# Attention units ahead of two mixture stages: other banks, bias engines and issue order in the first twenty units

## The chip, the cores and the metric

The kernel runs on one core of a Trainium2 chip. The metric is the device time of one execution in microseconds (us). The program is launched once; loads from HBM and the write of the result count.

## The reference, cut to what matters

Three layers follow each other. The change touches the first and the start of the second.

```python
# 1. attention: 4 batches, 8 heads, 576 positions, 64 wide, window 128, ALiBi bias
scores = q @ k.T / 8 + bias[h]            # bias[h] = -slope[h] * distance, masked outside the window
attn = exp(scores - max); attn /= sum(attn) + 1e-9
x = (attn @ v)                            # becomes 2304 tokens x 512
# 2. gated layer
x = (sigmoid(x @ w_gate) * (x @ w_val)) @ w_out        # 512 -> 1536 -> 512
# 3. top-1 mixture of 8 experts
out = gate_w * (relu(x @ w1[e]) @ w2[e])
```

## The kernel before, in words

The attention is cut into 36 **units**: a unit is two heads (one pair `g`) by two blocks of 128 tokens (`b`, `b+1`). The chunks of tokens are 2, 4, 4, 4 and 4 blocks (`CHUNKS`), so units 0 to 3 are chunk 0, units 4 to 11 chunk 1, units 12 to 19 chunk 2, and so on. A unit goes through these functions:

- `unit_s` (line 204): eight score products into two banks of tag `s`, then for each of four slices z VectorE adds the bias and takes the row's minimum (L225), and ScalarE takes the exponential with its sum (L228).
- `unit_n` (line 232): VectorE makes the reciprocal of the sums (L238, L239), and GpSimd scales the four slices (L108); for units 0 and 1 VectorE takes half of them (L106).
- `unit_t` (line 245): TensorE transposes the scaled slices into two banks (L255), and two copies take them to SBUF (`tt`): ScalarE the one of u = 0 (L96), VectorE the one of u = 1 (L98).
- `unit_b` (line 274): the products with v go to one bank `o` (L288); a copy (`xf`, VectorE for units below 11 and ScalarE from then on) takes the result to SBUF.
- `bias_of` (line 148) makes a head's bias tile from `relm` when it is first asked for, by a ScalarE multiplication (L154). `make_edge` (line 185) builds, for the units that hold a batch's edge, four masked copies of bias tiles on GpSimd (L100 and L201).

There are eight PSUM banks: two of tag `s`, two of `t`, three of `m` and one of `o`. In the first twenty units (`NA = 20`) transposes use `t` and the product with v uses `m`. From unit 20 on the product with v uses the single bank `o`, and `m` belongs to the gated layer.

The gated layer is computed for the pairs of chunks by seven products each (`seven`, line 392: m1 to m7 on sums and differences of blocks of x and of the weights), and for chunk 0 ("rest") by two classical products, `rg` (gate) and `rv` (value) in `rest_mm` (L451), of twelve matmuls each. Every operand is split into a high and a low part: a ScalarE copy (L96), then a VectorE subtraction (L112). Weights arrive as 64-bit words and are turned into float32 by one ScalarE and three VectorE instructions per half (L116, L122, L123, L125), then summed (L353 to L356) and split.

The order of the work: `with tc.manual_schedule(engines=...)` makes the named engines issue in source order; the engines that are not named get their order from the framework's scheduler, which sees the dependences and the source's order as a priority. Lines 491 to 514 name TensorE, VectorE, ScalarE and GpSimd. Twelve idle products (`warm`, L493) come first, then units 0 to 2, then a loop over i = 0 to 20 in which iteration i issues `unit_t(i)`, `unit_b(i-1)`, `unit_n(i+2)`, `make_edge(i+5)`, `unit_s(i+3)`, loads, and whatever the table `AT` holds for i: from i = 5 on the splits, sums and weight conversions of the gated layer. From line 540 on, for units 20 to 35, only TensorE is named; each iteration also runs some steps of the gated layer, taken from the list `todo` (line 517), each with the weight work (`after`) that follows it. SP issues the loads and has an order of its own throughout.

Of the kernel before, what the change touches and what calls it, by code (L numbers as in the profile page):

```python
# [15 lines left out]
ALU = mybir.AluOpType  # L16
# [5 lines left out]
B, H, S, D = 4, 8, 576, 64  # L22
# [5 lines left out]
P = 128  # L28
# [3 lines left out]
KF = FF // P  # L32
# [11 lines left out]
NWARM = 12  # L44
CHUNKS = [2, 4, 4, 4, 4]
PAIRS = [(2, 1), (4, 3)]
NA = 20
LEAD = 3
UB = 5
STEPS = [2, 4, 4, 5] + [5] * 12  # L50

# [2 lines left out]
def attn_ffn_moe(ctx: ExitStack, tc: tile.TileContext, qd, kd, vd, wgv, w_out, emb, tau, w1, w2, cst, ids, out):  # L54
    nc = tc.nc
# [15 lines left out]
    def pt(tag, name, bufs):  # L71
        return ps.tile([P, 512], F32, tag=tag, name=name, bufs=bufs)
# [9 lines left out]
    relm = cs[:, 0:256]  # L82
# [65 lines left out]
    def bias_of(h):  # L148
        while len(bias_t) <= h:
            z = len(bias_t)  # L150
            if z % 4 == 0:
                bias_c.append(slot([P, 4, 256], F32, f"bias{z}"))
            t = bias_c[-1][:, z % 4, :]
            nc.scalar.mul(t, relm, -8.0 * 2.0 ** (-8.0 * (z + 1) / H))  # L154
            bias_t.append(t)
        return bias_t[h]

# [5 lines left out]
    def load_qk(i):  # L163
        if i >= NU or i in qk_t:
            return
        c, b, g = units[i]
        lo = 0 if b else P
        q = ap.tile([P, 256], F32, tag="q", name=f"q{i}", bufs=UB)
        k = ap.tile([P, 384], F32, tag="k", name=f"k{i}", bufs=UB)
        nc.sync.dma_start(q, qd[:, g, b * P:b * P + 256])  # L170
        nc.sync.dma_start(k[:, lo:384], kd[:, g, (b - 1) * P + lo:(b + 2) * P])
        qk_t[i] = (q, k)
# [31 lines left out]
    def unit_s(i):  # L204
        if i >= NU or i in has_s:
            return
        has_s.add(i)
        c, b, g = units[i]
        fks = [first_key(b + j) for j in range(2)]
        halves = [slice(u * D, u * D + D) for u in range(2)]  # L210
        q, k = qk_t[i]
        ss = [pt("s", f"s{i}_{u}", 2) for u in range(2)]
        for j, f in enumerate(fks):
            for u in range(2):
                nc.tensor.matmul(ss[u][:, j * 256 + f:j * 256 + 256], q[halves[u], j * P:(j + 1) * P],  # L215
                                 k[halves[u], j * P + f:j * P + 256], start=True, stop=True)
        p = ap.tile([P, 4, 256], F32, tag="p", name=f"p{i}", bufs=4)
        mx = ap.tile([P, 4], F32, tag="mx", name=f"mx{i}", bufs=4)
        su = ap.tile([P, 4], F32, tag="su", name=f"su{i}", bufs=4)
        for u in range(2):  # L220
            for j, f in enumerate(fks):
                z = 2 * u + j
                bias = edge.pop((i, u, j), None)
                bias = bias_of(2 * g + u) if bias is None else bias
                nc.vector.tensor_tensor_reduce(  # L225
                    out=p[:, z, f:], in0=ss[u][:, j * 256 + f:j * 256 + 256], in1=bias[:, f:],
                    scale=-0.125, scalar=3.0e38, op0=ALU.add, op1=ALU.min, accum_out=mx[:, z:z + 1])
                nc.scalar.activation(out=p[:, z, f:], in_=p[:, z, f:], func=AF.Exp, scale=-1.0,  # L228
                                     bias=mx[:, z:z + 1], accum_out=su[:, z:z + 1])
        fst[i] = (p, fks, su)  # L230
# [14 lines left out]
    def unit_t(i):  # L245
        p, fks, su = fst[i]
        tts = []
        for u in range(2):
            t = pt("t", f"t{i}_{u}", 2)
            tt = ap.tile([P, 512], F32, tag="pt", name=f"tt{i}_{u}", bufs=4)  # L250
            runs = []
            for j, f in enumerate(fks):
                for o in range(f, 256, P):
                    a = j * 256 + o
                    nc.tensor.transpose(t[:, a:a + P], p[:, 2 * u + j, o:o + P], ident)  # L255
                    if runs and runs[-1][1] == a:
                        runs[-1][1] = a + P
                    else:
                        runs.append([a, a + P])
            for a, z in runs:  # L260
                hi_copy("v" if u and i < NA else "a", tt[:, a:z], t[:, a:z])
            tts.append(tt)
        fst[i] = (tts, fks)
# [10 lines left out]
    def unit_b(i):  # L274
        c, b, g = units[i]
        tts, fks = fst.pop(i)
        v = v_t.pop(i)
        o = pt("m", f"o{i}", 3) if i < NA else pt("o", f"o{i}", 1)
        mms = []
        for kb in range(-1, 2):  # L280
            q0, q1 = max(kb, 0), min(kb + 2, 2)
            if kb < 1 and fks[kb + 1]:
                q1 = min(q1, kb + 1)
            if q1 > q0:
                mms.append((kb, q0, q1, (kb + 1 + q0) * P))
        for z, (kb, q0, q1, c0) in enumerate(mms):
            for u in range(2):
                nc.tensor.matmul(o[u * D:u * D + D, q0 * P:q1 * P], v[:, kb + 1, u * D:u * D + D],  # L288
                                 tts[u][:, c0:c0 + (q1 - q0) * P], start=(z == 0), stop=(z == len(mms) - 1),
                                 skip_group_check=True)  # L290
        x = x_of(c, b, g)
        return lambda: hi_copy("v" if i < 11 else "a", x, o[:, 0:256])
# [14 lines left out]
    def builds(pair):  # L307
        one, two = PAIRS[pair]

        def src(half, k):  # L310
            return xf[PAIRS[pair][half], k]

        return {
            "S1+": lambda: sum_x((pair, "S1"), src(1, 0), src(1, 1), ALU.add),
            "S3+": lambda: sum_x((pair, "S3"), src(1, 0), src(0, 0), ALU.subtract),
            "S2+": lambda: sum_x((pair, "S2"), xf[pair, "S1"], src(0, 0), ALU.subtract),
            "S4+": lambda: sum_x((pair, "S4"), src(0, 1), xf[pair, "S2"], ALU.subtract),
            "A11": lambda: split_x((pair, "A11"), src(0, 0)),
            "A12": lambda: split_x((pair, "A12"), src(0, 1)),
            "A22": lambda: split_x((pair, "A22"), src(1, 1)),  # L320
            "S1": lambda: split_x((pair, "S1"), xf[pair, "S1"]),
            "S2": lambda: split_x((pair, "S2"), xf[pair, "S2"]),
            "S3": lambda: split_x((pair, "S3"), xf[pair, "S3"]),
            "S4": lambda: split_x((pair, "S4"), xf[pair, "S4"]),
        }
# [43 lines left out]
    def split_w(pair, f, z):  # L369
        if f < KF:  # L370
            t = (wf, tf)[z].pop(f)
            h_, l_ = (wide([P, 2 * KD, P], f"w{y}{pair}{z}_{f}", pair or f < 10) for y in "hl")
            hi_copy("a", h_, t)
            lo_sub("v", l_, t, h_)
            for q, name in enumerate((("B11", "B21", "B12", "B22"), ("T1", "T2", "T3", "T4"))[z]):
                wq[pair, f, name] = (h_[:, 2 * q:2 * q + 2], l_[:, 2 * q:2 * q + 2])
# [98 lines left out]
    wp = pt("o", "warm", 1)  # L475
# [3 lines left out]
    def latest(*engines):  # L479
        traced = nc.cur_bb.bb.instructions  # L480
        return [next(i for i in reversed(traced) if i.engine == e) for e in engines]

    bA = builds(0)
    AT = {
        5: [lambda: split_x("rest", xf.pop((0, 0)))],
        12: [bA["S1+"]], 13: [bA["A22"], lambda: load_w(0)], 14: [bA["S1"], lambda: conv_w(0, 0)],
        15: [lambda: conv_w(0, 1), lambda: load_w(1)], 16: [lambda: sum_w(0)],
        17: [bA["A11"], lambda: split_w(0, 0, 0)], 18: [bA["S3+"], lambda: split_w(0, 0, 1)],
        19: [bA["S3"], bA["S2+"]], 20: [bA["S2"]],
    }  # L490
    with tc.manual_schedule(engines={ENG.PE, ENG.DVE, ENG.Activation, ENG.Pool}):
        for _ in range(NWARM):
            nc.tensor.matmul(wp, warm[:, 0:P], warm, start=True, stop=True)  # L493
        unit_s(0)
        unit_s(1)
        load_qk(4)
        load_qk(5)
        unit_n(0)
        unit_s(2)
        load_qk(6)  # L500
        unit_n(1)
        for i in range(NA + 1):
            if i < NA:
                unit_t(i)
            if i:
                unit_b(i - 1)()
                load_v(i + 3)
            if i < NA:
                unit_n(i + 2)
                make_edge(i + 5)  # L510
                unit_s(i + LEAD)
                load_qk(i + LEAD + 4)
            for t in AT.get(i, []):
                t()
# [1 line left out]

    todo = []
    for f in range(KF):
        s = seven(0, f, "mmm", True)
        steps = [s[z] for z in "m1 m2 m5 m6 rg m7 rv m4 m3".split()]  # L520
        if f == 0:
            steps = [s[z] for z in "m1 m5 rg m6 rv m7 m2 m4 m3".split()]
        after = {0: lambda f=f: load_w(f + 2), 1: lambda f=f: conv_w(f + 1, 0), 3: lambda f=f: conv_w(f + 1, 1),
                 4: lambda f=f: sum_w(f + 1), 5: lambda f=f: split_w(0, f + 1, 0), 7: lambda f=f: split_w(0, f + 1, 1)}
        for z, t in enumerate(steps):
            todo.append((t, after.get(z)))

# [620 lines left out]
```

## Time and profile before

| what | value |
|---|---|
| median of 3 runs | 864.5 us (863.77 to 866.05) |
| profiled execution, its own time | 864.99 us |
| its span, first to last instruction | 863.1 us |
| mean granted TensorE clock | 0.981 of full speed |
| TensorE busy | 824.4 us (96%) |
| VectorE busy | 552.7 us (64%) |
| ScalarE busy | 459.7 us (53%) |
| GpSimd busy | 174.9 us (20%) |
| DMA | 140.39 MB, 163 GB/s in the mean |

The span is what the instructions cover; the time of the execution is 1.9 us more. In the trace PE is TensorE's matmuls, PEld its weight loads, DVE VectorE, ACT ScalarE, POOL GpSimd and SP the queue that issues loads. Busy time of PE is modelled, since matmuls overlap, so it is an upper bound of its work. The granted clock is given as a share of 2.4 GHz; 0.5 is the lower of its two levels, 1.2 GHz.

### The profile page before, as it was taken

How to read it: one execution, taken by the hardware profiler on the slowest of the kernel's cores; microseconds unless marked ns; L12 is line 12 of the kernel's file. 1: busy time of each engine (PE TensorE's matmuls, PEld its weight loads, DVE VectorE, ACT ScalarE, POOL GpSimd, SP SyncE). 2: the span in 40 equal slices, each digit the busy share in tenths (PEclk: the TensorE clock that was granted, in tenths of full speed). 3: DMA queues.
4: the chain of work that ended last, by engine and by line, in shares of the span. 5: the costliest groups of instructions: out<-in, count | busy, mean ns of one | idle time of the engine just before them, and what ended most of it. 6: DMA issues, size and time to landing. Idle time of an engine off the chain costs nothing. (4 is left out here: it accounts for less than half of the span.)

```text
span 863.1 us, 13488 instructions
## 1 busy us (share of the span) xinstructions
PE 824.4 (96%) x4616; PEld 663.7 (77%) x4616; DVE 552.7 (64%) x1367; ACT 459.7 (53%) x937; POOL 174.9 (20%) x275
## 2 busy tenths in 40 slices
PE   7896889999999999999999999999999999999997
PEld 4664567788788888888777777777878989878885
DVE  4887798768678778778944445564745545545553
ACT  5785776667556456566654445554344334333331
POOL 2773652323200000000000101111221221320210
PEclk7997899999999999999999999999999999999999
DMA  5557466645256356666625544414456544444520
GB/s 176 149 164 227 119 214 223 221 165 201 80 204 219 128 197 228 215 235 227 221 62 153 163 130 122 122 50 111 158 172 205 176 164 170 156 156 151 178 78 17
DMA packets 72455, 140.39 MB, mean 163 GB/s; under 512 B 8984, under 2 KB 38296, under 8 KB 72386
## 3 DMA queue, kind: packets, MB, share of 16 engines
q1 hardware_dynamic: 68482, 129.41, 46.0%
q0 software_dynamic: 3904, 10.12, 3.7%
q8 instruction: 37, 0.61, 0.3%
q14 instruction: 32, 0.26, 0.1%
HBM read 103.23 MB, written 36.93 MB: 162 GB/s over the span
## 5 line engine op out<-in xcount | busy, mean ns | idle before, releaser
L725 PE MATMUL y<-wo,gh 128*128 128x512 f32 x432 | 141.6, 402 | 0.0
L108 POOL TENSOR_SCALAR p<-p,rs 128x256 f32<-128x256 f32 (+1 forms) x140 | 81.4, 600 | 131.5 <-DVE rs L239 72.9
L905 PE MATMUL h<-xe,weh 128*128 128x256 f32 (+4 forms) x512 | 105.8, 301 | 1.5 <-DVE h L908 1.5
L921 PE MATMUL z<-weh,h 128*128 128x512 f32 (+3 forms) x320 | 103.0, 399 | 0.0
L725 PEld LDWEIGHTS y<-wo,gh 128*128 128x128 f32 x432 | 79.9, 188 | 20.3 <-issue 3.3
L228 ACT ACTIVATE p<-p,mx 128x256 f32<-128x256 f32 (+1 forms) x144 | 69.9, 486 | 39.7 <-DVE mx L225 39.5
L112 DVE TENSOR_TENSOR wel<-wer,weh 128x1024 fp32r<-128x1024 f32 x64 | 78.1, 1223 | 20.1 <-ACT weh L96 19.8
L905 PEld LDWEIGHTS h<-xe,weh 128*128 128x128 f32 x512 | 83.2, 188 | 4.2 <-DVE h L908 2.7
L725 PE MATMUL y<-wo,gl 128*128 128x512 f32 x216 | 85.8, 398 | 0.0
L907 ACT ACTIVATE h<-h 128x256 fp32r<-128x256 f32 (+4 forms) x64 | 26.6, 417 | 96.6 <-PE h L905 95.0
L905 PE MATMUL h<-xe,wel 128*128 128x256 f32 (+4 forms) x256 | 76.2, 299 | 0.3 <-DVE wel L112 0.2
L96 ACT CAST weh<-wer 128x1024 fp32r<-128x1024 f32 x64 | 66.2, 1048 | 8.3 <-DMA wer<-in_w 8.2
L921 PEld LDWEIGHTS z<-weh,h 128*128 128x128 f32 (+3 forms) x320 | 56.7, 180 | 15.0
L921 PE MATMUL z<-wel,h 128*128 128x512 f32 (+3 forms) x160 | 63.2, 395 | 0.0
L926 POOL DMA_INDIRECT out<-y,cols x19 | 25.0, 1315 | 172.0 <-DVE y L925 159.9
L255 PE MATMUL t<-cs,p 128*128 128x128 f32 x272 | 41.6, 294 | 13.6 <-ACT tt L96 6.9
L908 DVE SCALAR_TENSOR_TENSOR h<-h,h 128x256 fp32r<-128x256 f32 (+4 forms) x64 | 29.6, 464 | 38.0 <-ACT h L907 37.8
L925 DVE TENSOR_SCALAR y<-z,xg 128x512 f32<-128x512 f32 (+3 forms) x22 | 16.5, 749 | 57.4 <-PE z L921 54.2
L255 PEld LDWEIGHTS t<-cs,p 128*128 128x128 f32 x272 | 32.8, 150 | 24.8 <-issue 16.4
L819 POOL DMA_INDIRECT tab_d<-ids_sb,ai x18 | 18.3, 1017 | 163.1 <-DVE ai L816 139.6
L741 ACT ACTIVATE xr<-y 128x512 f32<-128x512 f32 x18 | 10.8, 598 | 76.0 <-PE y L725 68.7
L215 PE MATMUL s<-k,q 64*128 64x256 f32 (+1 forms) x288 | 46.1, 428 | 3.9 <-DVE mx L225 3.9
(327 smaller groups left out, 1949.4 us busy)
## 6 DMA issues: line engine op xcount, KB each, us to landing
wer<-in_w SPq DMA_DIRECT2D x64, 512.0 KB, 4.7
gl<-gT_d SPq DMA_DIRECT2D x27, 512.0 KB, 6.1
wr<-in_wgv SPq DMA_DIRECT2D x24, 512.0 KB, 5.2
gT_d<-c SPq DMA_DIRECT2D x48, 256.0 KB, 2.1
k<-in_kd SPq DMA_DIRECT2D x32, 192.0 KB, 2.8
v<-in_vd SPq DMA_DIRECT2D x32, 192.0 KB, 2.4
wf_d<-wf SPq DMA_DIRECT2D x12, 512.0 KB, 2.7
tf_d<-tf SPq DMA_DIRECT2D x12, 512.0 KB, 2.9
```

The costliest lines, as they stand in the source:

```text
L96: nc.scalar.copy(o, i)
L108: nc.gpsimd.tensor_scalar(out=t, in0=t, scalar1=r, scalar2=0.0, op0=ALU.mult, op1=ALU.add)
L112: e.tensor_tensor(out=o, in0=i, in1=h.bitcast(F32), op=ALU.subtract)
L215: nc.tensor.matmul(ss[u][:, j * 256 + f:j * 256 + 256], q[halves[u], j * P:(j + 1) * P], k[halves[u], j * P + f:j * P + 256], start=True, ...
L228: nc.scalar.activation(out=p[:, z, f:], in_=p[:, z, f:], func=AF.Exp, scale=-1.0, bias=mx[:, z:z + 1], accum_out=su[:, z:z + 1])
L255: nc.tensor.transpose(t[:, a:a + P], p[:, 2 * u + j, o:o + P], ident)
L725: nc.tensor.matmul(m, g[:, k % 4, u * P:(u + 1) * P], w[:, k % 3, :], start=(k == 0 and z == 0), stop=(k == KF - 1 and z == 2))
L905: nc.tensor.matmul(m[:, :n], w[:, fs], x[:, k, :], start=(cnt == 0), stop=(cnt == 3 * KD - 1))
L907: nc.scalar.activation(out=hh, in_=m[:, :n], func=AF.Relu)
L908: nc.vector.scalar_tensor_tensor(out=hl, in0=m[:, :n], scalar=0.0, in1=hh.bitcast(F32), op0=ALU.max, op1=ALU.subtract)
L921: nc.tensor.matmul(m[0:w, :], h, ww[:, ds], start=(cnt == 0), stop=(cnt == 3 * KE - 1))
L926: nc.gpsimd.indirect_dma_start(out=out, out_offset=IOA(ap=idx[0:w], axis=0), in_=y[0:w, :], in_offset=None, bounds_check=NT - 1, oob_is_er ...
```

## The change

Five edits are made, all in the attention units and at the start of the gated layer.

1. Transposes of the odd units below 20 take their two banks from tag `m` (three banks); even units keep `t`. The product with v takes the single bank `o` in every unit.
2. All eight bias tiles are made ahead of unit 0: head 0's on ScalarE, head 1's on VectorE, heads 2 to 7 on GpSimd.
3. Fourteen more idle products stand behind the scores of units 0, 1 and 2 (4, 4 and 6), into the bank `o` that the twelve first ones use.
4. `rg` and `rv` of the gated layer's first weight block move from the list `todo` (units 21 and 22) to iterations 19 and 20. The list has two steps fewer, and the weight work that hung on them hangs on their neighbours.
5. From iteration 10 (`SPLIT`) to 20 only TensorE and GpSimd issue in source order; VectorE and ScalarE are ordered by the scheduler there, as they were from unit 20 on.

```diff
+SPLIT = 10
...
-            nc.scalar.mul(t, relm, -8.0 * 2.0 ** (-8.0 * (z + 1) / H))
+            s = -8.0 * 2.0 ** (-8.0 * (z + 1) / H)
+            if z == 0:
+                nc.scalar.mul(t, relm, s)
+            elif z == 1:
+                nc.vector.tensor_scalar_mul(t, relm, s)
+            else:
+                nc.gpsimd.tensor_scalar(out=t, in0=relm, scalar1=s, scalar2=0.0, op0=ALU.mult, op1=ALU.add)
...
-            t = pt("t", f"t{i}_{u}", 2)
+            t = pt("m", f"t{i}_{u}", 3) if i < NA and i % 2 else pt("t", f"t{i}_{u}", 2)
...
-        o = pt("m", f"o{i}", 3) if i < NA else pt("o", f"o{i}", 1)
+        o = pt("o", f"o{i}", 1)
...
+    sA = [seven(0, f, "mmm", True) for f in range(KF)]
...
-        19: [bA["S3"], bA["S2+"]], 20: [bA["S2"]],
+        19: [bA["S3"], bA["S2+"], sA[0]["rg"]], 20: [bA["S2"], sA[0]["rv"]],
...
-        for _ in range(NWARM):
-            nc.tensor.matmul(wp, warm[:, 0:P], warm, start=True, stop=True)
+        def keep_warm(n):
+            for _ in range(n):
+                nc.tensor.matmul(wp, warm[:, 0:P], warm, start=True, stop=True)
+
+        keep_warm(NWARM)
+        bias_of(H - 1)
         unit_s(0)
+        keep_warm(4)
         unit_s(1)
+        keep_warm(4)
         load_qk(4)
         load_qk(5)
         unit_n(0)
         unit_s(2)
+        keep_warm(6)
         load_qk(6)
         unit_n(1)
-        for i in range(NA + 1):
+        for i in range(SPLIT):
...
+    with tc.manual_schedule(engines={ENG.PE, ENG.Pool}):
+        for i in range(SPLIT, NA + 1):
...
-            steps = [s[z] for z in "m1 m5 rg m6 rv m7 m2 m4 m3".split()]
+            steps = [s[z] for z in "m1 m5 m6 m7 m2 m4 m3".split()]
...
+        if f == 0:
+            after = {z: after[y] for z, y in enumerate((0, 1, 3, 4, 5, 7))}
```

The two loops hold the same calls as the one loop before.

## Rows read from the trace of the kernel before

**Rows 1.** The profile's first two parts: busy time, and the span in 40 slices.

```profile
PE 824.4 (96%) x4616; PEld 663.7 (77%) x4616; DVE 552.7 (64%) x1367; ACT 459.7 (53%) x937; POOL 174.9 (20%) x275
...
PE   7896889999999999999999999999999999999997
...
PEclk7997899999999999999999999999999999999999
```

**Rows 2.** Stretches: length, busy time and instructions of PE, PEld, DVE, ACT, POOL; clock, DMA.

```profile
0.00:20.00 20.00, 14.87 (x60) 8.31 (x62) 8.54 (x52) 11.38 (x39) 4.33 (x14) 0.79 0.63 187
20.00:50.00 30.00, 26.81 (x222) 18.66 (x218) 24.42 (x103) 22.01 (x78) 23.61 (x63) 0.97 0.49 143
50.00:97.00 47.00, 36.57 (x276) 25.31 (x274) 35.97 (x131) 32.63 (x110) 23.46 (x48) 0.82 0.60 184
97.00:115.00 18.00, 14.47 (x106) 10.90 (x105) 14.53 (x38) 13.35 (x32) 10.35 (x17) 1.00 0.43 128
115.00:180.00 65.00, 61.76 (x383) 49.24 (x383) 52.65 (x136) 44.55 (x110) 22.40 (x41) 0.97 0.67 222
180.00:863.00 683.00, 669.95 (x3579) 551.27 (x3577) 416.57 (x915) 335.75 (x571) 90.72 (x94) 1.00 0.48 157
```

**Rows 3.** The same view for two stretches at the lower clock.

```profile
12.30:22.20 9.90, 9.87 (x43) 6.51 (x43) 6.48 (x31) 6.55 (x26) 5.75 (x15) 0.53 0.39 116
69.00:79.70 10.70, 8.26 (x48) 5.55 (x45) 6.63 (x24) 7.45 (x24) 3.19 (x8) 0.52 0.71 223
```

**Rows 4.** The bias tiles: all of L154, one wait in the timeline, all such waits.

```profile
L154 ACT ACTIVATE bias<-cs x8: 398/400/416, 4.9 to 19.0; 128x256 f32<-128x256 f32 x8
...
8.31 0.29 DVE L225 CUSTOM_DVE_ANT_0 p<-s,bias 128x128 f32<-128x128 f32 x1 [1.01 <-ACT bias L154]
...
DVE p L225 <- ACT bias L154: 5.1, 5, 1.0
```

**Rows 5.** The timeline of POOL from unit 2's scaling to unit 10's, and its groups there.

```profile
17.96 1.64 POOL L108 TENSOR_SCALAR p<-p,rs 128x128 f32<-128x128 f32 x4 [0.54 <-DVE rs L239]
...
45.58 3.69 POOL L108 TENSOR_SCALAR p<-p,rs 128x256 f32<-128x256 f32 x8
...
L108 POOL TENSOR_SCALAR p<-p,rs 128x256 f32<-128x256 f32 (+1 forms) x36 | 16.2, 472 | 4.6 <-PE t L255 2.5 <-DVE rs L239 2.1
L100 POOL TENSOR_SCALAR edge<-bias 128x256 f32<-128x256 f32 x16 | 6.5, 408 | 0.7
L201 POOL MEMSET edge<- 64x192 f32 (+1 forms) x16 | 3.2, 203 | 0.9
```

**Rows 6.** Idle products at the start: weight loads, in the timeline.

```profile
4.15 0.15 PEld L493 LDWEIGHTS <-warm 128*128 128x128 bf16 x1 [0.28 <-issue]
...
4.58 0.57 PEld L493 LDWEIGHTS <-warm 128*128 128x128 bf16 x3 [0.28 <-issue]
```

**Rows 7.** Transposes of units 5, 10 and 20 in the timeline; their group, 50.3 to 97.1.

```profile
31.43 1.09 PE L255 MATMUL t<-cs,p 128*128 128x128 f32 x8 [0.16 <-ACT tt L96]
...
50.31 1.06 PE L255 MATMUL t<-cs,p 128*128 128x128 f32 x8 [0.19 <-ACT tt L96]
...
97.11 0.66 PE L255 MATMUL t<-cs,p 128*128 128x128 f32 x4
...
L255 PE MATMUL t<-cs,p 128*128 128x128 f32 x72 | 12.4, 308 | 10.4 <-ACT tt L96 4.5 <-DVE rs L238 4.0 <-issue 1.5
```

**Rows 8.** Unit 23 in the timeline: its scores, its scaling, and unit 21's product with v.

```profile
103.17 1.14 PE L215 MATMUL s<-k,q 64*128 64x256 f32 x8
...
111.80 4.11 POOL L108 TENSOR_SCALAR p<-p,rs 128x256 f32<-128x256 f32 x4 [6.87 <-DVE rs L239]
111.91 1.09 PE L288 MATMUL o<-tt,v 128*64 128x128 f32 x12 [2.31 <-ACT xf L96]
```

**Rows 9.** Two neighbouring matmuls of `rg` in the timeline.

```profile
106.72 0.28 PE L451 MATMUL r<-xl_rest,wh 128*128 128x256 f32 x1
...
106.84 0.28 PE L451 MATMUL r<-xh_rest,wl 128*128 128x256 f32 x1
```

More of the change, by code (lines that the diff above doesn't have):

```diff
@@ L499, in attn_ffn_moe @@
         unit_s(2)
+        keep_warm(6)
         load_qk(6)
         unit_n(1)
-        for i in range(NA + 1):
+        for i in range(SPLIT):
+            if i < NA:
+                unit_t(i)
+            if i:
+                unit_b(i - 1)()
+                load_v(i + 3)
+            if i < NA:
+                unit_n(i + 2)
+                make_edge(i + 5)
+                unit_s(i + LEAD)
+                load_qk(i + LEAD + 4)
+            for t in AT.get(i, []):
+                t()
+    with tc.manual_schedule(engines={ENG.PE, ENG.Pool}):
+        for i in range(SPLIT, NA + 1):
             if i < NA:
@@ L518, in attn_ffn_moe @@
     for f in range(KF):
-        s = seven(0, f, "mmm", True)
+        s = sA[f]
         steps = [s[z] for z in "m1 m2 m5 m6 rg m7 rv m4 m3".split()]
         if f == 0:
-            steps = [s[z] for z in "m1 m5 rg m6 rv m7 m2 m4 m3".split()]
+            steps = [s[z] for z in "m1 m5 m6 m7 m2 m4 m3".split()]
         after = {0: lambda f=f: load_w(f + 2), 1: lambda f=f: conv_w(f + 1, 0), 3: lambda f=f: conv_w(f + 1, 1),
                  4: lambda f=f: sum_w(f + 1), 5: lambda f=f: split_w(0, f + 1, 0), 7: lambda f=f: split_w(0, f + 1, 1)}
+        if f == 0:
+            after = {z: after[y] for z, y in enumerate((0, 1, 3, 4, 5, 7))}
         for z, t in enumerate(steps):
```

## The prediction, made before the changed kernel was run

> **What bounds the kernel now.** I read the page's slices first, then the time by stage, then the timeline of the weak stages. TensorE is busy 824.4 of 863.1 us, and the slices show that the missing part lies at the front, where the granted clock dips too [rows 1]. By stage: before 115 us PE is busy 92.7 of 115 us and idle 22.3; in the 65 us behind it idles 3.2, and from 180 us on 13 in 683 [rows 2]. So behind 115 us the kernel is bound by TensorE and what remains is a fixed amount of work: a microsecond by which that stage begins earlier is a microsecond off the end, unless DVE, busy 52.7 of 65 us there, can't keep up. All five edits lie ahead of that point. Two stretches at the lower clock add to the loss: around 17 us PE is busy 9.87 of 9.9 us at a clock of 0.53, around 74 us 8.26 of 10.7 at 0.52 [rows 3]; behind gaps in PE's work, both.
>
> Durations are those of the profiled execution, 864.99 us; the median is 0.5 less. I sum against 865.0 and take 0.5 off. A measurement of this kernel tells 0.3%, 2.6 us, from no change.
>
> **The start: biases, idle products and banks, up to unit 10.** ScalarE makes eight biases of 0.40 us, one at a time between its exponentials, and VectorE's first score of a head waits 1.01 us for one, 5.1 us in five waits [rows 4]. Made ahead, six of them cost POOL 0.41 each by its like instruction of the same shape, 2.5 us [rows 5], in a stretch where it is busy 4.3 of 20 us [rows 2]; the one on VectorE I bound by nothing and by ScalarE's 0.40, beside its wait for the first scores, and take nothing. The first of the five waits ends at 8.31, the last stands near 19; four lie ahead of unit 2's scaling at 17.96. They are 4 x 1.01 = 4.0 us of a chain in which scores, exponentials and the next unit's scores follow each other, so that scaling should start near 14.0.
>
> From there to unit 10's scaling POOL is the chain: it ends at 45.58 + 3.69 = 49.27, 31.3 us for 16.2 + 6.5 + 3.2 = 25.9 us of work, idle 5.4 [rows 5]. A part of it is what the new banks go at: transposes held by the last unit's ScalarE copy (PE's matmul 0.16 to 0.19 us in units 5 and 10 [rows 7]), since with two banks the next unit can't begin before both copies, and the scores and products queued behind them on PE. Four banks in turn take that wait away; the single `o` is late next, but below unit 10 its copy stands on VectorE ahead of the next scores, and one unit's transposes lie between. I let half of the idle time go, 2.5 us, so the start is worth 6.5 us. Upper bound: 4.0 with all of POOL's idle time but 1.6, 7.8. Lower bound: the fourteen idle products. The weight loads of the first ones stand 0.43 us apart, the last three lie within 0.57 us together, 0.19 each [rows 6]. At 0.19 they are 2.7 us, in the 5.1 us that PE is idle in the first 20 [rows 2]; at 0.43 they are 6.0, stand ahead of units 1's and 2's scores and of unit 0's transposes, and the 3.4 us more come off the 4.0. With no gain in POOL's idle time either, 0.6 is left. I take the quick price, since the twelve first ones end on it.
>
> **Free order, iterations 10 to 20.** Units 10 to 20 take 97.1 - 50.3 = 46.8 us [rows 7], 4.68 a unit where units 5 to 10 took (50.3 - 31.4) / 5 = 3.8. VectorE is busy 36.0 us of it and ScalarE 32.6 [rows 2]: in source order the splits and conversions stand as blocks between units, each engine waits for the other's half, and PE's transposes wait 10.4 us in sum [rows 7]. Freed, the blocks fill holes. What it can give at most is VectorE's idle time, 47.0 - 36.0 = 11 us. What it costs shows in unit 23, in the stage where both engines are free already: from its scores at 103.17 to the end of its scaling at 111.80 + 4.11 = 115.9 it takes 12.7 us [rows 8], because splits go between its four slices. Scores run three units ahead, so such a unit allows a period of 12.7 / 3 = 4.24 us: 42.4 in place of 46.8, a gain of 4.4. I take 4.5, the end nearer to a row of the very mechanism; the range keeps 0 and 11. The SP loads of q, k and v are tied to PE's order and not moved.
>
> In that unit POOL's four scalings take 4.11 us where the mean of four is 4 x 0.47 = 1.9 [rows 5, 8]. Without the stretch the unit's chain would be 10.5 us and the period 3.5: a gain of 11.7, VectorE's whole bound.
>
> By the Trainium skill, page "SBUF — State Buffer", section "Who interferes with whom", a VectorE instruction with two SBUF inputs and a GpSimd one that reads SBUF exclude each other for a whole instruction. By that the stretch stays wherever splits are put beside scalings, and the sum goes by 4.5 and not by 11; the stretched row agrees, and it speaks against this edit.
>
> **rg and rv.** Their 24 matmuls stand 0.12 us apart [rows 9], 2.9 us of PE's work, moved from between products of unit 21 and 22 into iterations 19 and 20. PE is idle 3.5 us from 97 to 115 [rows 2]. Where they go they fill gaps; where they were they covered the wait for the splits of S2 and S3, which m6 and m7 now meet at once. So between 0 and 2.9; I take 1. The weight work moves with the steps and changes no engine's total.
>
> **Sum.** 6.5 + 4.5 + 1 = 12 us: 865.0 - 12 - 0.5 = **852.5 us**. By the lower ends (0.6, 0, 0) 864, by the upper ones (7.8, 11, 2.9) 843.
>
> **Rivals.**
>
> *POOL holds the free units.* If each scaling is stretched to 4.11 us and the edges of units 21, 23, 25 and 27 come beside them, built in iterations 16, 18, 20 and 22, POOL has 2 x 4.11 + 2.8 = 11 us for two units, 5.5 a unit. (Four edges are 4 x (0.41 + 0.20) = 2.4 by the groups, 2.8 with gaps [rows 5].) Units 16 to 19 then lose 4 x (5.5 - 4.24) = 5 us, and the free part gives nothing: 865 - 6.5 - 1 - 0.5 = 857; with the start at its lower bound 863. For it: one row of 4.11. Against it: POOL is busy only 23.5 of 47 us there [rows 2].
>
> *The one bank o makes it slower.* From unit 11 on the copy that frees `o` is ScalarE's; freed, it may stand behind exponentials and splits. In the stage where that is so already, PE waits 2.31 us for it with unit 21's product [rows 8]. PE issues in source order, so the next scores and transposes queue behind the waiting product. Ten units of that are 23.1 us; the 10.4 us that PE idles now [rows 7] absorb a part, 12.7 remain. With the start's 6.5 kept and no other gain: 865 + 12.7 - 6.5 - 0.5 = 871. It turns slower than before once the waits exceed the present idle time by 9 us (6.5 + 2.6), 0.9 a unit. Against it: with little to fill in, the copy is short and old in the source's order, and only some waits behind 97 us are of that size.
>
> *The order doesn't change.* The scheduler, following source priority, may give nearly the old order between 50 and 97 us: the free part is then nothing, 857.
>
> *VectorE fills wholly.* Its bound of 11 us is nearly reached: 843 to 846.
>
> **Chances and range.** The forecast, 846 to 857: 0.55. POOL, 857 to 863: 0.25, of which 0.05 lies within 0.3%. Order unchanged, 857: 0.05. VectorE filled: 0.03. One bank: 0.12, of which 0.02 within 0.3%. So faster by over 0.3%: 0.55 + 0.20 + 0.05 + 0.03 = 0.83; within: 0.07; slower: 0.10. The range reaches over the forecast and POOL's case, a little above its upper end and the sum's lower bounds: 844 to 864. Left out are the bank's case and part of VectorE's.
>
> **What would show it.** In the changed profile the waits of VectorE for a bias should be gone, unit 2's scaling should start near 14 us and unit 10's end near 42.8; the granted clock should stay at its upper level between 10 and 22 us. Unit 20's transposes should start near 97.1 - 11 = 86 us, and the work behind 115 us should be the same, begun some 12 us earlier. Wrong would be: a clock of 0.5 in the start with the idle products 0.43 apart; scalings of 4 us throughout iterations 10 to 20; waits of PE's product with v on the copy of `o`, ten times over; or an early start that the stage behind 115 us loses again in waits of PE on VectorE.

## The result and the profile after

The changed kernel takes 853.32 us in the median of four runs (852.27 to 854.88), the kernel before beside it 864.83 (863.77 to 866.05): a ratio of 0.9866 with a 95% interval of 0.9847 to 0.9884, 11.5 us less. 852.5 was forecast, in a range of 844 to 864. The sum came out; several of its terms did not, and the experiments below take them apart. The profiled execution after is the slowest of the four, 854.88 us with a span of 852.9.

The page of the changed kernel, the parts that answer to [rows 1]:

```profile
PE 827.9 (97%) x4630; PEld 663.3 (78%) x4630; DVE 550.7 (65%) x1368; ACT 456.4 (54%) x930; POOL 184.3 (22%) x281
...
PE   9998898999999999999999999999999999999997
...
PEclk9999899999999999999999999999999999999999
```

The hole at the front is smaller, and of the clock's dips one still shows in the slices. The time by stage of the changed kernel, with the columns of [rows 2]:

```profile
0.00:20.00 20.00, 18.78 (x107) 10.19 (x108) 11.92 (x66) 11.59 (x43) 9.11 (x29) 1.00 0.73 214
20.00:50.00 30.00, 28.23 (x215) 18.98 (x213) 23.30 (x98) 21.17 (x73) 22.95 (x59) 0.94 0.48 143
50.00:97.00 47.00, 43.36 (x314) 30.30 (x314) 38.28 (x138) 37.38 (x120) 32.21 (x54) 0.89 0.58 187
97.00:115.00 18.00, 15.66 (x88) 11.27 (x86) 15.76 (x39) 13.23 (x32) 7.80 (x15) 1.00 0.56 179
```

Before 115 us PE is busy 106.0 in place of 92.7 us, and the clock of the first 20 us is 1.00 in place of 0.79. The whole of the first 180 us in one row each, for the kernel before, the changed kernel and e5, the changed kernel without two of its edits (below):

```profile
0.00:180.00 180.00, 154.47 (x1039) 112.43 (x1040) 136.11 (x452) 123.93 (x367) 84.16 (x181) 0.91 0.59 186
...
0.00:180.00 180.00, 168.42 (x1114) 120.38 (x1115) 140.53 (x467) 127.00 (x368) 97.40 (x191) 0.96 0.60 193
...
0.00:180.00 180.00, 164.43 (x1141) 119.73 (x1142) 145.19 (x479) 131.52 (x382) 98.22 (x199) 0.99 0.63 199
```

Milestones of the changed kernel from its timeline, beside [rows 5, 7]: unit 2's scaling, unit 10's scaling, then the first transposes of units 10 and 20 and the second half of unit 20's:

```profile
15.22 1.63 POOL L109 TENSOR_SCALAR p<-p,rs 128x128 f32<-128x128 f32 x4 [0.54 <-DVE rs L246]
...
43.55 1.84 POOL L109 TENSOR_SCALAR p<-p,rs 128x256 f32<-128x256 f32 x4 [0.57 <-DVE rs L246]
...
46.26 0.33 PE L262 MATMUL t<-cs,p 128*128 128x128 f32 x1
...
83.55 0.48 PE L262 MATMUL t<-cs,p 128*128 128x128 f32 x1
...
92.28 0.71 PE L262 MATMUL t<-cs,p 128*128 128x128 f32 x4
```

In the kernel before, unit 19's first transposes and the second half of unit 20's:

```profile
90.45 0.87 PE L255 MATMUL t<-cs,p 128*128 128x128 f32 x3 [2.40 <-ACT tt L96]
...
98.59 0.63 PE L255 MATMUL t<-cs,p 128*128 128x128 f32 x4
```

Unit 2's scaling comes 2.7 us earlier, unit 10's ends 49.27 - 45.39 = 3.9 earlier, its transposes start 4.0 earlier. Unit 20's first transposes start 13.6 earlier, but that is not the same point of the work: where the order is free, half of them are issued ahead of and among unit 22's scores, and the kernel before issues them behind. Their second half starts 98.59 - 92.28 = 6.3 earlier, with `rg` now ahead of it as a product that before stood later. Three places in this trace lose again. In the first, between 34 and 40 us, unit 7's transposes run at once, and PE then has nothing until the product with v of unit 6 can go. From the timeline:

```profile
33.25 1.29 PE L262 MATMUL t<-cs,p 128*128 128x128 f32 x8
36.16 1.09 PE L295 MATMUL o<-tt,v 128*64 128x128 f32 x12 [1.61 <-issue]
37.18 2.70 PE L222 MATMUL s<-k,q 64*128 64x256 f32 x8
39.81 1.77 PE L262 MATMUL t<-cs,p 128*128 128x128 f32 x8
...
35.65 0.41 DVE L99 COPY xf<-o 128x256 f32<-128x256 f32 x1
```

Two stretches of 2 us around it, with the columns of [rows 2]:

```profile
34.00:36.00 2.00, 0.55 (x4) 0.20 (x2) 2.00 (x4) 0.27 (x1) 0.05 (x1) 1.00 0.62 191
...
38.00:40.00 2.00, 2.00 (x7) 1.17 (x8) 1.79 (x9) 1.58 (x6) 1.79 (x6) 0.50 0.33 98
```

The product starts 0.10 us after the copy `xf` that frees the one bank `o` (35.65 + 0.41 = 36.06). PE is busy 0.55 of the 2 us ahead, and from 38 to 40 us the granted clock is 0.50: the scores behind take 2.70 us and the next transposes 1.77, where 1.14 and 1.09 are their times elsewhere at the upper level [rows 7, 8]. In the second place POOL is late, and `rg` runs behind it at the lower clock. The timeline, and then the stretch around it:

```profile
78.14 6.29 POOL L109 TENSOR_SCALAR p<-p,rs 128x256 f32<-128x256 f32 x8
...
81.64 0.33 PE L262 MATMUL t<-cs,p 128*128 128x128 f32 x1 [0.87 <-POOL p L109]
...
88.32 0.41 PE L458 MATMUL r<-xl_rest,wh 128*128 128x256 f32 x1
...
88.54 0.42 PE L458 MATMUL r<-xh_rest,wl 128*128 128x256 f32 x1
```

```profile
83.00:93.00 10.00, 10.00 (x48) 7.09 (x45) 6.33 (x16) 5.68 (x15) 6.65 (x11) 0.53 0.18 54
```

Eight scalings take 6.29 us, 3.1 for four where [rows 5] have 1.9; `rg`'s matmuls stand 0.21 us apart where [rows 9] have 0.12, in a stretch with a clock of 0.53. The third place is m7's first matmul, which waits for ScalarE's copy of the bank that m6 filled, a wait that the same matmul does not have in the trace of before (115.5 us), where `rv` stands between them:

```profile
103.97 0.50 PE L392 MATMUL a<-xh_(0, 'S3')_1349,wh 128*128 128x512 f32 x1 [2.22 <-ACT r L432]
```

### The profile page after: what moved, and what is told of

It is laid out like the page before. It is cut to its first block, busy times and chain, and to the rows that moved or that the text cites. A ratio compares the mean times of both kernels' runs of the same rounds, so it can differ in the third digit from the quotient of the medians.

```text
span 852.9 us, 13498 instructions
## 1 busy us (share of the span) xinstructions
PE 827.9 (97%) x4630; PEld 663.3 (78%) x4630; DVE 550.7 (65%) x1368; ACT 456.4 (54%) x930; POOL 184.3 (22%) x281
## 5 line engine op out<-in xcount | busy, mean ns | idle before, releaser
L109 POOL TENSOR_SCALAR p<-p,rs 128x256 f32<-128x256 f32 (+1 forms) x140 | 88.4, 649 | 111.0 <-DVE rs L246 35.9
L952 PEld LDWEIGHTS z<-weh,h 128*128 128x128 f32 (+3 forms) x320 | 56.7, 180 | 14.9
L936 PEld LDWEIGHTS h<-xe,wel 128*128 128x128 f32 x256 | 48.1, 188 | 0.7 <-DVE wel L113 0.7
L232 DVE CUSTOM_DVE_ANT_0 p<-s,bias 128x256 f32<-128x256 f32 (+1 forms) x112 | 40.0, 398 | 12.6 <-PE s L222 12.4
```

The costliest lines, as they stand in the source:

```text
L109: nc.gpsimd.tensor_scalar(out=t, in0=t, scalar1=r, scalar2=0.0, op0=ALU.mult, op1=ALU.add)
L232: nc.vector.tensor_tensor_reduce(out=p[:, z, f:], in0=ss[u][:, j * 256 + f:j * 256 + 256], in1=bias[:, f:], scale=-0.125, scalar=3.0e38, o ...
L936: nc.tensor.matmul(m[:, :n], w[:, fs], x[:, k, :], start=(cnt == 0), stop=(cnt == 3 * KD - 1))
L952: nc.tensor.matmul(m[0:w, :], h, ww[:, ds], start=(cnt == 0), stop=(cnt == 3 * KE - 1))
```

## The experiments

Each kernel was timed in five rounds against the kernel before on its chip. Intervals are those of the ratio to the kernel before, whose medians were 864.2 to 865.1 us.

| kernel | what it is | median, us | ratio, 95% interval |
|---|---|---|---|
| changed | all five edits | 853.3 | 0.9866 (0.9847 to 0.9884) |
| e1 | changed, all in source order | 862.3 | 0.9965 (0.9947 to 0.9982) |
| e2 | before + free order | 855.5 | 0.9880 (0.9862 to 0.9898) |
| e3 | before + biases and idle products | 858.0 | 0.9919 (0.9904 to 0.9933) |
| e4 | changed less the move of rg, rv | 854.4 | 0.9870 (0.9851 to 0.9889) |
| e5 | e4 less the bank edit | 849.5 | 0.9822 (0.9808 to 0.9837) |
| e6 | changed less the idle products | 852.4 | 0.9857 (0.9840 to 0.9874) |
| e7 | changed less the biases | 852.6 | 0.9876 (0.9848 to 0.9904) |
| e8 | changed, m2 between m6 and m7 | 850.6 | 0.9829 (0.9809 to 0.9849) |
| e9 | e8 less the bank edit | 847.6 | 0.9794 (0.9770 to 0.9818) |
| e10 | e4 with six idle products more | 850.1 | 0.9837 (0.9809 to 0.9866) |
| e11 | e5 less the biases | 853.7 | 0.9870 (0.9847 to 0.9893) |
| e12 | changed less the bank edit | 850.3 | 0.9817 (0.9800 to 0.9834) |

**Source order again (e1).**

```diff
-SPLIT = 10
+SPLIT = 21
```

> The changed kernel with all four engines in source order up to iteration 20 (the split at 21). Theory of the three terms: free order is worth 4 to 5 us of the 11.5, so this takes 857.5 to 858.5 us, and its units 10 to 20 take 46 to 47 us again. Rival, the front's shift and the banks are all: the blocks between units cost nothing once four banks are there, and this takes 853 to 854, like the changed kernel.

862.29 us, of twelve runs nine at 861.2 to 864.1 and three at 857.3 to 857.7. By the medians free order is worth 9.0 us to the changed kernel, twice the term; and the other four edits together gain 2.8, less than biases and idle products alone do in e3. Neither theory had that: some edit costs. It does not cost in every execution: the three quick runs, the profiled one among them, are as quick as e3. Their mean granted clock is 0.988 to 0.992, that of the nine 0.985 or 0.986.

**Free order alone (e2).** The kernel before, its loop cut at 10, and the second part under `engines={ENG.PE, ENG.Pool}`.

> The kernel before with one edit: VectorE and ScalarE free of source order from iteration 10 on. Theory of the three terms: 860 us (4 to 5 gained) with no help from the other edits. Rival, free order only pays with four banks and an early start: 863.5 to 866, no change.

855.47 us, 9.6 less: more than the first theory had, and with no help from the other edits. Its stretch from 50 to 97 us, and then its timeline (first transposes of units 10, 19 and 20, second half of unit 20's; scores and scaling of unit 18):

```profile
50.00:97.00 47.00, 41.94 (x341) 29.89 (x342) 42.20 (x155) 40.80 (x131) 35.52 (x59) 1.00 0.67 211
```

```profile
50.12 1.06 PE L256 MATMUL t<-cs,p 128*128 128x128 f32 x8 [0.19 <-ACT tt L97]
...
82.48 1.25 PE L256 MATMUL t<-cs,p 128*128 128x128 f32 x5 [0.36 <-POOL p L109]
...
85.89 0.33 PE L256 MATMUL t<-cs,p 128*128 128x128 f32 x1
...
89.11 0.66 PE L256 MATMUL t<-cs,p 128*128 128x128 f32 x4
...
68.96 1.14 PE L216 MATMUL s<-k,q 64*128 64x256 f32 x8
...
76.70 2.80 POOL L109 TENSOR_SCALAR p<-p,rs 128x256 f32<-128x256 f32 x4 [1.88 <-DVE mx L226]
```

From unit 10's transposes to unit 19's it takes 82.48 - 50.12 = 32.4 us, 3.60 a unit, against 90.45 - 50.31 = 40.1, 4.46 a unit, before. By unit 20's first transposes the gain would be 46.8 - 35.8 = 11.0 us, but half of them are issued early here; by their second half it is 98.59 - 89.11 = 9.5. VectorE is busy 42.2 us between 50 and 97 where [rows 2] have 36.0, and the clock is 1.00 there in place of 0.82. Unit 18 takes 76.70 + 2.80 - 68.96 = 10.5 us from scores to scaled, a third of which is 3.5.

**The start alone (e3).** Edits 2 and 3 of the five, on the kernel before.

> The kernel before with two edits: biases ahead on three engines, and the fourteen idle products. Theory of the three terms: units 4 to 10 come 3 to 4 us earlier and that reaches the end, 861 us. Rival, the source-ordered blocks of units 10 to 20 and the clock swallow an early start: 863.5 to 865.5.

858.03 us, 7.1 less. Both numbers are missed, the rival's by far. In its trace unit 20 starts 4.5 us earlier (92.6 in place of 97.1). Some 1.5 us more come where the trace of before has a stretch at the lower clock, from 138 to 142 us, and this one has none: from unit 25 on the lead is 6.0. The last 1.6 of the 7.6 by which the two profiled executions differ come behind the attention units; their cause is open.

**rg and rv back (e4).**

```diff
-        19: [bA["S3"], bA["S2+"], sA[0]["rg"]], 20: [bA["S2"], sA[0]["rv"]],
+        19: [bA["S3"], bA["S2+"]], 20: [bA["S2"]],
...
-            steps = [s[z] for z in "m1 m5 m6 m7 m2 m4 m3".split()]
+            steps = [s[z] for z in "m1 m5 rg m6 rv m7 m2 m4 m3".split()]
...
-        if f == 0:
-            after = {z: after[y] for z, y in enumerate((0, 1, 3, 4, 5, 7))}
```

> The changed kernel with rg and rv back in the list, between m5 and m6 and between m6 and m7. Theory of the three terms: 1 us slower than the changed kernel, 854.3. Rival, m7 now waits 2.66 us for the copy of m6's bank that rv covered and rg runs at the lower clock: 851 to 852.5, faster than the changed kernel.

854.41 us, in five runs from 850.9 to 855.4. The median is what the first theory said; the intervals of e4 and of the changed kernel cover each other, so the run decides nothing on a term of 1 us.

**Biases, idle products and free order, without banks and move (e5).** e4, and:

```diff
-            t = pt("m", f"t{i}_{u}", 3) if i < NA and i % 2 else pt("t", f"t{i}_{u}", 2)
+            t = pt("t", f"t{i}_{u}", 2)
...
-        o = pt("o", f"o{i}", 1)
+        o = pt("m", f"o{i}", 3) if i < NA else pt("o", f"o{i}", 1)
```

> The changed kernel without the bank edit and without the move of rg and rv: biases, idle products and free order alone. The two parts alone gained 7.1 (biases and idle products) and 9.6 us (free order); with them the changed kernel gained 11.5 and not 16.7. Theory A, the parts overlap (both fill the same lost clock and the same slack behind 80 us): 853 to 855. Theory B, they add and the banks or the moved products take 5 us back: 848 to 850.

849.54 us (848.8 to 850.0), faster than the changed kernel with intervals apart. Theory B holds by the time: free order adds 858.0 - 849.5 = 8.5 us to the start, the start 855.5 - 849.5 = 6.0 to free order, and banks and move take 3.8 back. Where unit 7's transposes stand in its timeline, and then the stretch of the time by stage:

```profile
34.04 0.63 PE L262 MATMUL t<-cs,p 128*128 128x128 f32 x4 [1.09 <-ACT tt L97]
35.53 0.63 PE L262 MATMUL t<-cs,p 128*128 128x128 f32 x4 [0.86 <-DVE tt L99]
36.09 1.09 PE L295 MATMUL o<-tt,v 128*64 128x128 f32 x12
```

```profile
20.00:50.00 30.00, 26.67 (x232) 18.90 (x232) 24.32 (x106) 22.39 (x76) 22.92 (x59) 1.00 0.51 149
```

With two banks the halves of the transposes wait 1.09 and 0.86 us in turn, for the copies of the unit ahead; unit 6's product with v starts at 36.09, as in the changed kernel at 36.16. The wait that the bank edit removes was not on the path: it only lay spread. The clock of the whole stretch stays at 1.00 in this execution, where the changed kernel's has 0.94; e12 shows that this is not a matter of the banks alone.

**No idle products (e6).** All three calls of `keep_warm` behind the first are taken out.

> The changed kernel without the fourteen idle products. Theory A, they hold the upper clock in the start: without them a stretch of 10 us at half clock comes back near 11 us and costs 2 to 3 us in units 0 to 3, 855.5 to 856.5 in the end. Theory B, faster biases alone keep PE busy enough, or TensorE isn't the bound there: 852 to 854, no change.

852.40 us, theory B. Its first stage, and then unit 2's scaling from its timeline:

```profile
0.00:20.00 20.00, 17.18 (x94) 9.50 (x94) 12.05 (x66) 11.95 (x45) 9.36 (x29) 1.00 0.76 217
```

```profile
14.96 1.63 POOL L109 TENSOR_SCALAR p<-p,rs 128x128 f32<-128x128 f32 x4 [0.54 <-DVE rs L246]
```

With the biases out of the way the clock stays at 1.00 without them, and unit 2's scaling is no later than with them: 14.96 against 15.22, where the eight other traces with early biases have 13.8 to 14.9.

**Biases back on ScalarE (e7, e11).** In e7 in the changed kernel, in e11 in e5.

```diff
-            s = -8.0 * 2.0 ** (-8.0 * (z + 1) / H)
...
+            nc.scalar.mul(t, relm, -8.0 * 2.0 ** (-8.0 * (z + 1) / H))
...
-        bias_of(H - 1)
```

> The changed kernel with the biases back on ScalarE, each made when first asked for; idle products kept. Theory A, the biases are the 4 us of the start: unit 2's scaling near 18 us again, 857 in the end. Theory B, the clock is what the start gains and the biases are hidden: 853 to 854.5.

> Idle products and free order alone: the kernel with 849.5 us, with the biases back on ScalarE, made when first asked for. Theory A, the biases are 4 us of the start and reach the end: 853 to 854. Theory B, the start's gain was the clock, which the idle products alone hold: 849.5 to 851.

e7 took 852.56 us, four runs at 851.2 to 852.9 and two at 857.6 and 859.4: by the time theory B, since the interval holds 853 to 854.5 and not 857. In its trace the biases do cost: the transposes of units 10 and 19 start 2.5 us later than in the changed kernel's. But it has no stretch at the lower clock near 85 us, and the second half of unit 20's starts 2.0 us earlier. So late biases cost, and in this pair something else takes the cost back. e11, without the bank edit, took 853.70 against e5's 849.54, with intervals apart: there the biases are worth 4.2 us at the end, theory A. e11's unit 2 scales where the kernel before does (17.96), with a clock of 1.00 in its first stage (the timeline, then the time by stage):

```profile
17.82 1.63 POOL L109 TENSOR_SCALAR p<-p,rs 128x128 f32<-128x128 f32 x4 [0.54 <-DVE rs L240]
```

```profile
0.00:20.00 20.00, 16.00 (x82) 7.85 (x82) 8.65 (x52) 11.53 (x41) 4.43 (x15) 1.00 0.65 190
```

So idle products alone hold the clock there too, as the biases alone do in e6; one of the two is enough.

**m2 ahead of m7 (e8), and that without the bank edit (e9).**

```diff
-            steps = [s[z] for z in "m1 m5 m6 m7 m2 m4 m3".split()]
+            steps = [s[z] for z in "m1 m5 m6 m2 m7 m4 m3".split()]
```

> The changed kernel with m2 moved between m6 and m7 in the first weight block, so that ScalarE's copy of m6's bank is covered by a product again. Theory A, the 2.2 to 2.7 us that m7 waits for that copy come off the end: 851. Theory B, the wait only moves to another product of the same block, since the splits that feed them are late: 853 to 854.

> The changed kernel without the bank edit, and with m2 between m6 and m7; rg and rv stay in iterations 19 and 20. Theory A, the bank edit is what costs 4 to 5 us and the moved products are worth 1 to 2 once m7's wait is covered: 847.5 to 849, faster than biases, idle products and free order alone (849.5). Theory B, the moved products are worth nothing, covered or not: 849.5 to 851.

e8 took 850.63 us, 2.7 under the changed kernel, as theory A has it, though the two intervals touch by 0.0002. Its trace speaks for theory B. m7 no longer waits for the copy of m6's bank, but two other products of the block wait now, unit 21's with v and m4, which waits for the copy of m7's bank:

```profile
101.20 1.09 PE L295 MATMUL o<-tt,v 128*64 128x128 f32 x12 [1.68 <-ACT xf L97]
...
107.39 0.50 PE L392 MATMUL a<-xh_(0, 'A22')_980,wh 128*128 128x512 f32 x1 [2.44 <-ACT c L436]
```

What this execution has ahead of the changed kernel's is there before m2 comes: m1 starts at 90.67 in place of 94.27, without a stretch at the lower clock around 85 us. So a gain by the cover is not shown. e9 took 847.62 (846.3 to 849.0): theory A by the time, 17.4 us under the kernel before and 5.7 under the changed one, the lowest median of all kernels here. m4 waits 2.44 us in its trace too.

**The gap filled (e10).** e4, and behind `unit_t(7)`:

```diff
+            if i == 7:
+                wp = pt("t", "warm7", 2)
+                keep_warm(6)
```

> The changed kernel with rg and rv back in the list and all else kept, the bank edit too, and six more idle products behind the transposes of unit 7, in a bank of tag t; there PE waits 1.6 us without work for the copy that frees the one bank o, and the granted clock falls to half behind it. Without them it took 854.4. Theory A, the bank edit costs by this gap and the clock that falls behind it: no half clock between 34 and 45 us, and 850 to 851.5. Theory B, the edit costs by its waits for the one bank o all along: 853.5 to 855.

850.08 us, five of six runs at 849.0 to 850.8 and one at 855.6. Its timeline at the place, and then two stretches of 2 us:

```profile
33.89 1.46 PE L502 MATMUL warm<-warm 128*128 128x512 bf16 x6
35.62 1.09 PE L295 MATMUL o<-tt,v 128*64 128x128 f32 x12 [0.27 <-DVE xf L99]
```

```profile
36.00:38.00 2.00, 2.00 (x17) 1.25 (x14) 2.00 (x10) 1.74 (x7) 1.95 (x5) 1.00 0.11 18
38.00:40.00 2.00, 2.00 (x20) 1.43 (x19) 1.79 (x10) 1.58 (x6) 1.68 (x6) 1.00 0.45 140
```

The product with v still waits for the bank, now by name: VectorE's copy `xf`. But the clock stays at 1.00, and the scores behind take 1.80 us, in place of 2.70 in the changed kernel. The median is 4.3 us under e4's, and five of the six runs have a mean granted clock of 0.996 or 0.997 where e4's have 0.989 to 0.994. This is theory A by trace and median, and not beyond doubt: the intervals of e4 and e10 overlap (0.9851 to 0.9866), since each has runs of the other's size, and e4's profiled execution, with the half clock from 35 to 38 us in it, took 850.89 us, 1.9 more than e10's 848.97. So this one fall explains some 2 us, and the rest of the 4.3 lies in executions that have no trace. By the Trainium skill, page "TensorE: Matmul & The Clock Gate", section "What's actually happening", the throttled clock is the default and activity releases it; this pair of traces agrees, one execution each.

**Without the bank edit alone (e12).** The two lines of e5's diff, on the changed kernel.

> The changed kernel without the bank edit alone: rg and rv moved, m7 behind m6 with no product between. Theory A, the move gains PE's idle time early and gives it back in m7's wait of 2.2 to 2.7 us: 849 to 850.5, like 849.5 without the move, and 2 us over the 847.6 with m2 between. Theory B, the move is worth its 1 to 2 us without m2's help: 847.5 to 848.5.

850.25 us, theory A, with an interval apart from the changed kernel's: the bank edit by itself costs 3.1 us by the medians and 4.2 by the ratios (0.0049 of 865). Against e5, the same without the move, there is no difference (849.5; the intervals lie on each other), and e9 with m2 between is 2.6 us lower in the median, with intervals that overlap a little.

Its profiled execution, at 854.97 us the slowest of the five, corrects the reading of e5. The banks are those of before, and the transposes of unit 7 wait in two parts, as in e5. From the timeline, and then the 2 us behind:

```profile
33.44 0.63 PE L262 MATMUL t<-cs,p 128*128 128x128 f32 x4 [1.08 <-ACT tt L97]
34.91 0.63 PE L262 MATMUL t<-cs,p 128*128 128x128 f32 x4 [0.84 <-DVE tt L99]
...
36.00:38.00 2.00, 2.00 (x12) 1.26 (x10) 1.82 (x9) 2.00 (x9) 1.94 (x6) 0.50 0.00 0
```

The clock falls here without the bank edit. So it does at this place in e3 and e11: behind the two waits in three traces of seven without the edit, behind the one gap, where it is not filled, in five of six with it (e1's stays up). The second place is alike. Up to m6 e12 and e9 issue the same products, and POOL is late in both; the same 10 us of e12, then of e9:

```profile
80.00:90.00 10.00, 9.93 (x41) 6.73 (x43) 6.73 (x22) 5.00 (x13) 6.22 (x12) 0.51 0.21 59
...
80.00:90.00 10.00, 9.93 (x77) 7.66 (x79) 8.38 (x25) 8.23 (x23) 8.31 (x14) 1.00 0.28 77
```

PE is busy 9.93 us in both, and issues 41 matmuls in one execution and 77 in the other. A fall that one trace shows belongs to that execution first, and to the edit only if other traces agree.

## Why the prediction was right, and where it was not

**Sum: the close number is luck.** 12 us were forecast and 11.5 measured, but by errors that cancel: the free order was sized at half, the bank edit has the other sign, and the move shows no gain. The sum also has no term for the clock, though the text names two stretches at the lower level. In the rows of the first 180 us the clock is 0.91 and 0.96, which is some 16 and 7 us of full-speed time not granted: 9 us less, where the two profiled executions differ by 10.1. This is bookkeeping and not a cause: the gaps that the edits close stand ahead of falls of the clock, and no run changes the clock with all else left alone.

**Biases: right.** 4.0 us were taken, 4.2 reach the end (e11 against e5); e7 against the changed kernel does not show it at the end. Unit 2's scaling starts at 15.2 and not 14.0 in the changed kernel, between 13.8 and 15.0 in the nine other traces with early biases. In e11 the transposes start 3.7 us later than in e5 at unit 4 and 4.1 later at unit 10.

**Banks: the step that failed.** "Four banks in turn take that wait away" and "I let half of the idle time go, 2.5 us" is wrong in sign. With the edit the median is 3.1 us (the changed kernel against e12), 4.9 (e4 against e5) and 3.0 (e8 against e9) higher, the last with intervals that overlap. The wait of the transposes for the last unit's copies went, but they were not on the path: the product behind them on PE waits for VectorE's copies either way (36.09 in e5, 36.16 in the changed kernel). POOL's idle time stayed: from unit 2's scaling to the end of unit 10's the changed kernel takes 30.2 us, where the trace of before has 31.3 and the sum had 28.8. The single `o` was named as late next, but at the wrong price: the copy stands on VectorE ahead of the next scores, as the text said, and behind the split of "rest", which it did not say.

What the loss consists of is shown in part only. In these pairs the runs with the edit have the lower granted clock, in the mean 0.992, 0.992 and 0.993 against 0.995, 0.996 and 0.996; over 850 us that is some 2.6 to 3.4 us of full-speed time, an estimate near the loss itself. One fall was followed to the gap ahead of unit 6's product, and filling the gap took it away (e10). But the clock falls there without the edit too (e3, e11, e12), and e7, with the edit and late biases, ran at 0.996 and is no slower than e11, which has neither the edit nor the move. Why the clock falls more often with the edit stays open.

**Idle products: no gain where they were put.** The lower bound (they run at 0.43 and take 3.4 us of the 4.0) did not come, and nor did a gain: in e6 the clock of the first 20 us stays up without them.

**Free order: right in mechanism, mis-sized.** The term was 4.5 and is 8.5 (e5 against e3) to 9.6 (e2 alone). The step that failed was a period of 12.7 / 3 = 4.24 us, taken from unit 23; e2's units come every 3.60 us. Unit 18's 10.5 us over three gives 3.5, but one unit proves nothing: units 13 to 20 take 6.2 to 11.5 us from scores to scaled in e2, 9.2 in the mean, and a third of that is 3.1. In the kernel before it is 9.7, a third of which is 3.2, where units came every 4.46. So a unit's latency over the units in flight did not tell the period in either kernel. The blocks did fill holes, as the text said: VectorE's busy time there rose from 36.0 to 42.2 us. Its idle time, the upper bound of 11 us, was nearer to the answer than the period.

**The page's rule.** POOL's scalings are stretched beside VectorE's splits, sums and conversions, as the Trainium skill has it, page "SBUF — State Buffer", section "Who interferes with whom". In the first 180 us of the changed kernel's trace a scaling of 128x256 takes 0.48 us in the mean where it overlaps no TENSOR_TENSOR or SCALAR_TENSOR_TENSOR of VectorE (67 of them), and 0.97 us, at most 2.49, where it overlaps one (41). POOL is busy 32.2 in place of 23.5 us between 50 and 97. The stretch came, but its price of a larger period did not; the 4.5 that went by it was too low.

**rg and rv: no gain by themselves.** 1 us was taken; e12 against e5 shows none. The text looked for the cover at the splits of S2 and S3. The wait that came is for ScalarE's copy of the bank that m6 and m7 share, 2.2 us. m2 in that place moves the wait to m4 (2.44 us in e8 and e9). The move together with m2 is 849.5 - 847.6 = 1.9 lower in the medians of e5 and e9, with intervals that overlap.

**The rivals.** The bank edit did cost, but not by the rival's mechanism: in place of ten waits on ScalarE's copy from unit 11 on, the changed kernel's trace has one of 0.5 us up to 97 us, and one on VectorE's copy at unit 6. POOL's case is seen at 78 us alone. That the stage behind 115 us keeps an early start was right: in e5 unit 22's to unit 34's transposes all start 13.2 to 15.0 us earlier than before.

**Open.** Why the bank edit lowers the clock of most runs, and where. Why e3 gains 7.1 us where its unit 20 is 4.5 early was read from one trace, not tried. Nor was a filled gap at 80 us, where POOL is late.

## What to carry to other kernels

A wait that is removed pays only if what it held was on the path; if the next wait ends at the same moment, the same idle time is merely moved. Estimate a loosened order from the idle time of the engine that it fills, not from one unit's latency. Where a step is moved, look at what it stood between: the two steps on either side may share a bank. A profile is one execution: before a stretch at the lower clock is put down to an edit, look whether it stands in traces without the edit too. And compare two kernels at points where both have issued the same work.

## What the runs showed of the hardware that was not expected

Behind nearly the same waits of PE the granted clock fell to 0.50 in one execution and stayed at 1.00 in another: unit 7's two waits of 1.09 and 0.86 us in e5 and of 1.08 and 0.84 in e12, and the 10 us behind 80 in e12 and e9. In e10, 1.46 us of idle products in the gap go with a clock of 1.00 behind it. One kernel's scatter goes with the granted clock, and is wider than most single edits are worth: five runs of e12 go from 847.4 us at a mean granted clock of 0.997 to 855.0 at 0.989.
